# Six small unused transfers among the K and V loads of a one-core decode kernel

## The chip, the core and the metric

The kernel runs on one core of a Trainium2 chip. The metric is device time in microseconds (us). The kernel before was timed three times: 231.49, 231.35 and 231.1 us, so its median is 231.35 us.

## The reference

One token for each of two batch rows goes through a layer norm, and three things are added: the input, an attention with a cached window, and a gated feed-forward block.

```python
xn = _layernorm(x)                                   # x: 2 x 1 x 512
q  = xn @ wq                                         # 32 query heads of 128
k, v = last 4096 rows of k_cache, v_cache            # 2 x 8 heads x 4096 x 128, each for 4 query heads
p  = softmax(q @ k^T * 128 ** -0.5);  o = p @ v
h  = relu(xn @ W_gate) * (xn @ W_up)                 # 1792 wide
out = x + o @ wo + h @ W_down
```

All data is float32. The weights and the used part of the caches are 94.9 MB, each read once.

## The kernel before

Everything large comes through one issuing queue, SP's, in the order of the program text. The helper `load` (line 68) takes a tile from a ring of four slots of 128 x 32 KB and issues one transfer into it (line 70). In the order of its calls it loads: two halves of wq (calls 1 and 2), W_gate (3) and W_up (4), and then one pair of kv heads at a time, 4 MB each: K of group 0 in two parts (5 and 6), and from there K of group g and V of group g-1 by turns (7: K, 8: V, 9: K, 10: V, 11: K, 12: V, 13: K, and so on to call 20). A load waits until the slot that it takes is free, which is when TensorE has read the tile that was there, and until the transfer that filled that slot has landed.

After the loads come W_down (line 99, and two pieces of 128 KB, line 108, whose source pattern at line 106 has KX = 4 as its outermost count), one transfer of 4 MB for the first half of wo and four pieces of 2048, 1280, 512 and 256 KB for the second half (line 497). The program text fixes the order of the instructions on each engine: no scheduler moves them.

TensorE transposes each K tile in 64 steps of 128x128 (line 315), ScalarE and VectorE copy the results out of PSUM by turns (line 304), TensorE forms the scores (line 328). The softmax of the group before (line 334) is interleaved with the transposes of the next K tile, then the product with V follows (line 392). Four groups go through this. At the end W_down and wo are multiplied in as they land (line 479), the sum is copied (line 501) and stored (line 502).

A transfer of 128 rows is spread over the core's 16 DMA engines, here called load engines, eight rows on each. Each engine works through its share of the queue's transfers in order, and a transfer has landed when the last of its engines has finished its share.

Of the kernel before, what the change touches and what calls it, by code (L numbers as in the profile page):

```python
# [9 lines left out]
F32 = mybir.dt.float32  # L10
# [10 lines left out]
def kernel(  # L21
# [12 lines left out]
    nc = tc.nc  # L34
    P = 128
    B, _, D = x.shape
# [21 lines left out]
    const = ctx.enter_context(tc.tile_pool(name="const", bufs=1))  # L58
# [6 lines left out]
    ctx.enter_context(tc.manual_schedule())  # L65


    def load(name, src, shape):
        t = ring.tile(shape, F32, name=name, tag="ring")
        nc.sync.dma_start(t, src)  # L70
        return t


    def load_wq(m):
        src = wq[m * 2 * P:(m + 1) * 2 * P, :].rearrange("(p k) f -> p k f", p=P)
        return load(f"wq{m}", src, [P, 2, HQ * DH])

    def load_ff(w, name):
        return load(name, w.rearrange("(p k) f -> p k f", p=P), [P, KC, F])
# [34 lines left out]
    def load_kv(cache, name, g, a):  # L114
        r, b = divmod(g, B)
        base = cache[b, r * C + 2 * a, SK - W:SK, :]
        run = J * DH
        src = bass.AP(
            tensor=cache.tensor, offset=base.offset, ap=[[run, PK], [SK * DH, 2], [1, run]]
        )  # L120
        return load(f"{name}{g}_{a}", src, [P, run])
# [86 lines left out]
    for kc in range(KC):  # L208
        m, k = divmod(kc, 2)
# [321 lines left out]
```

## Time and profile before

| | us |
|---|---|
| median of three runs | 231.35 |
| the profiled execution | 231.31 |
| its span, first to last instruction | 229.5 |
| TensorE busy | 183.6 |
| VectorE busy | 67.3 |
| ScalarE busy | 48.6 |

The profiled execution takes 231.31 us, of which the span is 229.5 us; 1.81 us lie around it. Core clock: the granted TensorE clock is 0.948 on the mean. The page's DMA line gives, in 40 slices of the span, the busy share of the 16 load engines in tenths. The view by windows gives the same share for any stretch, so a share times 16 times the length of the stretch is load-engine time, and that divided by a count of packets is the time of one. A packet here is one row's piece of a transfer; the records also hold packets of 4 bytes, which post the completion of an engine's share.

### The profile page before, as it was taken

How to read it: one execution, taken by the hardware profiler on the slowest of the kernel's cores; microseconds unless marked ns; L12 is line 12 of the kernel's file. 1: busy time of each engine (PE TensorE's matmuls, PEld its weight loads, DVE VectorE, ACT ScalarE, POOL GpSimd, SP SyncE). 2: the span in 40 equal slices, each digit the busy share in tenths (PEclk: the TensorE clock that was granted, in tenths of full speed). 3: DMA queues.
4: the chain of work that ended last, by engine and by line, in shares of the span. 5: the costliest groups of instructions: out<-in, count | busy, mean ns of one | idle time of the engine just before them, and what ended most of it. 6: DMA issues, size and time to landing. Idle time of an engine off the chain costs nothing.

```text
span 229.5 us, 4147 instructions
## 1 busy us (share of the span) xinstructions
PE 183.6 (80%) x1876; PEld 114.8 (50%) x1876; DVE 67.3 (29%) x135; ACT 48.6 (21%) x82; POOL 7.7 (3%) x24
## 2 busy tenths in 40 slices
PE   0195754829999889998999799599999974988694
PEld 0151222429666573664584565348656533247582
DVE  0500101204544462441472341147224224001000
ACT  2000100004444561540252332025234202010000
POOL 8100000000000000000000000000000300000000
PEclk9999988976999999999999999979999997699889
DMA  7999999999999999999999999999999999999991
GB/s 275 451 428 408 455 405 443 423 448 434 405 443 440 421 411 445 437 417 431 434 440 415 445 417 425 434 428 434 420 445 425 423 428 432 413 448 420 414 367 54
DMA packets 3816, 95.15 MB, mean 415 GB/s; under 512 B 430, under 2 KB 438, under 8 KB 696
## 3 DMA queue, kind: packets, MB, share of 16 engines
q1 hardware_dynamic: 3796, 94.90, 96.7%
q8 instruction: 14, 0.23, 0.4%
q14 instruction: 2, 0.02, 0.0%
q10 hardware_dynamic: 4, 0.00, 0.0%
HBM read 94.90 MB, written 0.00 MB: 413 GB/s over the span
## 4 chain that ended last, share of the span: by engine, by line
PE 53%; DMA 34%; DVE 5%; POOL 2%; ACT 2%; issue 1%; SPq 0%; POOLq 0%
DMA k<-in_A_k_cache_dram 25%; PE pk L315 23%; PE s L328 11%; DMA wo<-in_A_wo_dram 10%; PE o L392 9%; PE q_ps L221 2%; PE pp L372 2%; PE xt_ps L211 2%; ACT p L361 2%; PE oa L408 2%; DVE kT L304 1%; PE y_ps L479 1%; PE op L422 1%; DVE on L304 1%; POOL spread L163 1%
## 5 line engine op out<-in xcount | busy, mean ns | idle before, releaser
L315 PE MATMUL pk<-ident,k 128*128 128x128 f32 x512 | 68.3, 287 | 7.3 <-DMA k<-in_A_k_cache_dram 7.3
L315 PEld LDWEIGHTS pk<-ident,k 128*128 128x128 f32 x512 | 58.1, 146 | 22.1 <-issue 17.9
L304 DVE COPY kT<-pk 128x512 f32<-128x512 f32 x64 | 44.3, 691 | 53.5 <-PE pk L315 43.6
L304 ACT COPY kT<-pk 128x512 f32<-128x512 f32 x64 | 37.5, 586 | 71.7 <-PE pk L315 71.7
L328 PE MATMUL s<-kT,qz 128*32 128x512 f32 x256 | 31.7, 610 | 0.0
L392 PE MATMUL o<-v,pt 128*32 128x512 f32 x256 | 31.6, 626 | 0.0
L392 PEld LDWEIGHTS o<-v,pt 128*32 128x32 f32 x256 | 11.2, 115 | 15.1 <-issue 10.4
L328 PEld LDWEIGHTS s<-kT,qz 128*32 128x32 f32 x256 | 7.2, 111 | 12.7 <-issue 12.3
L211 PE MATMUL xt_ps<-rep,xn 2*128 2x32 f32 x16 | 3.7, 400 | 10.4 <-DVE xn L205 10.4
L479 PE MATMUL y_ps<-wo,oT 128*17 128x128 f32 x256 | 9.5, 310 | 3.0 <-DMA wo<-in_A_wo_dram 3.0
L221 PE MATMUL q_ps<-wq,xnT 128*32 128x512 f32 x64 | 9.2, 727 | 3.3 <-DMA wq<-in_A_wq_dram 2.8
L408 PE MATMUL oa<-on,pick 128*16 128x128 f32 x64 | 8.3, 273 | 4.1 <-DVE on L304 3.3
L304 DVE COPY on<-o 128x512 f32<-128x512 f32 x4 | 2.8, 692 | 29.6 <-PE o L392 29.6
L408 PEld LDWEIGHTS oa<-on,pick 128*16 128x16 f32 x64 | 5.8, 97 | 11.1 <-DVE on L304 7.0
L479 PEld LDWEIGHTS y_ps<-wo,oT 128*17 128x17 f32 x256 | 7.9, 111 | 4.4 <-DMA wo<-in_A_wo_dram 3.9
L211 PEld LDWEIGHTS xt_ps<-rep,xn 2*128 2x128 f32 x16 | 3.6, 319 | 10.4 <-issue 10.4
L304 ACT COPY on<-o 128x512 f32<-128x512 f32 x4 | 2.3, 586 | 26.6 <-PE o L392 26.6
L98 POOL MEMSET wx<- 64x2048 f32 x1 | 1.8, 1804 | 174.5 <-PE s L328 174.5
L372 PE MATMUL pp<-ident,p 128*128 128x128 f32 x32 | 5.5, 306 | 2.4 <-ACT p L361 1.5
L361 ACT ACTIVATE p<-s,nm 128x1024 f32<-128x1024 f32 x4 | 4.5, 1115 | 12.5 <-DVE nm L356 12.5
L221 PEld LDWEIGHTS q_ps<-wq,xnT 128*32 128x32 f32 x64 | 2.2, 130 | 9.5 <-issue 5.2
L249 PE MATMUL g_ps<-wg,xnT 128*32 128x416 f32 x32 | 4.7, 752 | 2.6 <-DMA wg<-in_B_W_gate_dram 2.6
(84 smaller groups left out, 72.7 us busy)
## 6 DMA issues: line engine op xcount, KB each, us to landing
k<-in_A_k_cache_dram SPq DMA_DIRECT2D x8, 4096.0 KB, 28.9
v<-in_A_v_cache_dram SPq DMA_DIRECT2D x8, 4096.0 KB, 27.2
wq<-in_A_wq_dram SPq DMA_DIRECT2D x2, 4096.0 KB, 17.1
wo<-in_A_wo_dram SPq DMA_DIRECT2D x1, 4096.0 KB
wg<-in_B_W_gate_dram SPq DMA_DIRECT2D x1, 3584.0 KB, 29.8
wu<-in_B_W_up_dram SPq DMA_DIRECT2D x1, 3584.0 KB, 38.9
wd<-in_B_W_down_dram SPq DMA_DIRECT2D x1, 3328.0 KB
wo<-in_A_wo_dram SPq DMA_DIRECT2D x1, 2048.0 KB, 19.8
```

Source lines behind the costliest of these rows:

```text
L163: nc.gpsimd.tensor_copy(spread[:, e, :, e], ident[0:HR, 0:HR])
L211: nc.tensor.matmul(xt_ps[:, o, kc, :], cols, rep.rearrange("r s b -> r (s b)"), start=True, stop=True)
L221: nc.tensor.matmul(q_ps[r][32 * c:32 * c + 32, :], xnT[:, 0, kc, :], wqt[kc // 2][:, kc % 2, n * 512:(n + 1) * 512], start=(kc == 0), stop ...
L249: nc.tensor.matmul(dst[32 * c:32 * c + 32, :], xnT[:, 1, kc, :], wt[:, kc, c * MQ:(c + 1) * MQ], start=(kc == 0), stop=(kc == KC - 1),)
L304: (nc.vector.tensor_copy if turn[0] % 2 else nc.scalar.copy)(dst, src)
L315: nc.tensor.transpose(pk[:, u * P:(u + 1) * P], kt_in[:, j * P:(j + 1) * P], ident)
L328: nc.tensor.matmul(ss[g][32 * q:32 * q + 32, :], qz[:, g, 32 * n:32 * n + 32], kt[:, h, q * 512:(q + 1) * 512], start=(a == 0 and s1 == 0 ...
L361: nc.scalar.activation(p, both, AF.Exp, bias=nm, scale=SCALE, accum_out=l)
L372: nc.tensor.transpose(pp[:, u], pv[:, lo:lo + P], ident)
L392: nc.tensor.matmul(o[32 * q:32 * q + 32, :], pts[g][:, jh, n].rearrange("p u k -> p (u k)"), v[:, lo:lo + 512], start=(s1 == 0 and jh == 0 ...
L408: nc.tensor.matmul(oa[g], pick[:, u, 8 - 8 * a:24 - 8 * a], ons[a][:, u], start=(a == 0 and u == 0), stop=(a == NP - 1 and u == 3),)
L479: nc.tensor.matmul(y_ps[32 * e:32 * e + 17, :], lhsT.rearrange("p b s -> p (b s)")[:, 0:17], w[:, e * P:(e + 1) * P], start=False, stop=stop,)
```

## The change

`load` counts its calls. After each of calls 8 to 13 it allocates one more tile in the constant pool and issues one more transfer on the same queue, right behind the load. The six transfers take the first 128, 144, 160, 176, 192 and 208 elements (512, 576, 640, 704, 768 and 832 bytes) of the first 14, 12, 10, 8, 6 and 2 rows of W_down, and write each row to a partition of its own (0, 4, 8 and so on). By the change's description they run over 14, 12, 10, 8, 6 and 2 load engines. Nothing reads the six tiles. Together they are 52 rows and 32,384 bytes; they occupy 4,032 bytes of a partition.

```diff
+    at = [0]
+
     def load(name, src, shape):
         t = ring.tile(shape, F32, name=name, tag="ring")
         nc.sync.dma_start(t, src)
+        at[0] += 1
+        if 8 <= at[0] <= 13:
+            i = at[0] - 8
+            k = (14, 12, 10, 8, 6, 2)[i]
+            run = 128 + 16 * i
+            seen = const.tile([64, run], F32, name=f"seen{i}")
+            nc.sync.dma_start(
+                seen[0:4 * k:4, :], bass.AP(tensor=w_down.tensor, offset=w_down.offset, ap=[[D, k], [1, run]])
+            )
         return t
```

The instructions on TensorE, VectorE, ScalarE and GpSimd are the same ones in the same order; SP issues 35 transfers in place of 29. Completions are counted on eight semaphores taken by turns, so the six transfers move the later loads to other semaphores, and some instructions wait on a semaphore of another number. Where a semaphore comes round again, the next transfer waits for the one that had it: the fifth small transfer waits for the first, the sixth for the second, and calls 15, 17 and 19 and the W_down load wait for the third, fourth, fifth and sixth besides what they waited for before.

## The prediction

> **What bounds the kernel now.** I read the page's DMA row and its queue table first, then the view by windows in six stages and in the last microseconds, then SP's own timeline and waits. The load engines are busy from the second slice of the span to the last but one:
>
> ```profile
> PEclk9999988976999999999999999979999997699889
> DMA  7999999999999999999999999999999999999991
> ...
> q1 hardware_dynamic: 3796, 94.90, 96.7%
> q8 instruction: 14, 0.23, 0.4%
> ```
>
> SP's queue (q1) alone keeps 16 load engines occupied for 96.7% of 229.5 us, which is 221.9 us for each. TensorE, the next, is busy for 183.6 us. The view by windows (columns: stretch, length, busy time of each engine with its instruction count, granted clock, load engines' share, GB/s) says that this holds in every stage and is not only an average:
>
> ```profile
> 2.00:50.00 48.00, 25.22 (x280) 12.55 (x280) 7.50 (x29) 2.24 (x5) 4.47 (x17) 0.96 0.99 426
> 50.00:100.00 50.00, 47.64 (x389) 33.18 (x390) 23.17 (x37) 19.97 (x33) 0.00 (x0) 0.94 1.00 429
> 100.00:150.00 50.00, 44.34 (x380) 27.31 (x378) 17.22 (x30) 13.34 (x23) 0.00 (x0) 0.98 1.00 429
> 150.00:200.00 50.00, 44.50 (x368) 25.37 (x370) 17.78 (x34) 11.76 (x21) 1.80 (x1) 0.92 1.00 429
> ```
>
> From 50 to 200 us the share is 1.00 and the rate 429 GB/s, or 26.8 GB/s for each engine. So the engines never run dry, however long TensorE or SP wait, and time that is added to the busiest engine's work is not taken up by an idle stretch later. The chain of waits on the page gives TensorE 53% and transfers 34%; I do not go by it, because it follows a load back to its issue, and at its issue the engines still had earlier loads to finish.
>
> The end hangs on the load engines too. The drain and what follows it:
>
> ```profile
> 221.00:222.00 1.00, 1.00 (x45) 0.92 (x37) 0.00 (x0) 0.00 (x0) 0.00 (x0) 1.00 0.99 406
> 222.00:223.00 1.00, 1.00 (x47) 1.00 (x39) 0.00 (x0) 0.00 (x0) 0.00 (x0) 1.00 0.75 309
> 223.00:224.00 1.00, 0.32 (x12) 0.04 (x3) 0.00 (x0) 0.00 (x0) 0.00 (x0) 1.00 0.71 274
> 224.00:225.00 1.00, 0.85 (x32) 0.85 (x36) 0.00 (x0) 0.00 (x0) 0.00 (x0) 1.00 0.50 195
> 225.00:225.60 0.60, 0.60 (x24) 0.33 (x20) 0.00 (x0) 0.00 (x0) 0.00 (x0) 1.00 0.22 82
> ```
>
> ```profile
> 226.08 0.13 PEld L479 LDWEIGHTS y_ps<-wo,oT 128*17 128x17 f32 x8 [0.30 <-DMA wo<-in_A_wo_dram]
> 226.56 0.29 DVE L501 COPY yo<-y_ps 128x128 f32<-128x128 f32 x1 [12.30 <-PE y_ps L479]
> 226.88 0.61 SPq L502 DMA_DIRECT2D out_dram<-yo  x1
> ```
>
> The share falls from 0.99 to 0.22 within four microseconds: the 16 engines finish one after another, the first near 222 and the last near 225.5 us. The last eight matmuls (226.08) waited 0.30 us for the last piece of wo, and the copy and the store follow at once. So the time is set by the **latest** load engine, not by the mean of them. The idle share from 222 to 225.6 is (0.25 + 0.29 + 0.50 + 0.78 x 0.6), or 1.5 us for each engine: that is what evening out could give at most, and an engine that finishes early can take extra work for nothing.
>
> **The change part by part.** Nothing is removed. Added are 52 short rows on the load engines, six issues on SP, six tiles, and other semaphores.
>
> *The rows.* An engine gets at most one row of each transfer, so six at most (4,032 bytes) and none at least; the mean is 52/16 = 3.25 rows and 2,024 bytes. Rows this short are not loaded in the kernel before. The nearest packets are these: the 12 of the store (four of them of 4 bytes), in the DMA view of 228.0 to 228.3 us, and the last pieces of wo, in that of 225.0 to 225.6 us:
>
> ```profile
> DMA packets 12, 0.00 MB, mean 14 GB/s; under 512 B 4, under 2 KB 12, under 8 KB 12
> ...
> q1 hardware_dynamic: 12, 0.00, 5.4%
> ```
>
> ```profile
> DMA packets 31, 0.05 MB, mean 82 GB/s; under 512 B 7, under 2 KB 7, under 8 KB 31
> ...
> q1 hardware_dynamic: 31, 0.05, 22.3%
> ```
>
> The first: 5.4% of 16 x 0.3 us is 0.259 us over eight rows of 512 bytes, 0.032 us a row with its part of the completions; 512 bytes at 26.8 GB/s are 0.019 us, so 0.013 us is overhead. The second: 22.3% of 16 x 0.6 us is 2.14 us over 24 rows of 2 KB, 0.089 us a row. An engine with six rows therefore pays 4,032 bytes / 26.8 GB/s = 0.150 us and 6 x 0.013 = 0.08 us, together **0.23 us**. Bounds for one engine: 0 (it has no row) and 6 x 0.089 = 0.53 us (each row as dear as one of 2 KB). I take 0.23 us, since 512 bytes are nearer to these rows than 2 KB, and I let it count in full, as if the latest engine were one with five or six rows. The reason for that is in the code: the two W_down pieces have 4 as the outermost count of their source (line 106), so I take it that they load four engines with 64 KB each that the others do not have, 2.4 us at 26.8 GB/s, and that these are among the latest. If the latest has none of the rows, the change costs nothing there.
>
> [...] No view of the profile numbers the engines.
>
> *SP's issues.* A load's issue takes 0.53 to 0.54 us on SP; the six new ones stand right behind those of calls 8 to 13:
>
> ```profile
> 44.94 0.54 SPq L70 DMA_DIRECT2D v<-in_A_v_cache_dram  x1
> 60.90 0.54 SPq L70 DMA_DIRECT2D k<-in_A_k_cache_dram  x1
> 72.31 0.54 SPq L70 DMA_DIRECT2D v<-in_A_v_cache_dram  x1
> 86.89 0.54 SPq L70 DMA_DIRECT2D k<-in_A_k_cache_dram  x1
> 92.21 0.53 SPq L70 DMA_DIRECT2D v<-in_A_v_cache_dram  x1
> 101.94 0.54 SPq L70 DMA_DIRECT2D k<-in_A_k_cache_dram  x1
> 108.13 0.54 SPq L70 DMA_DIRECT2D v<-in_A_v_cache_dram  x1
> ```
>
> The shortest distance to the next load is 86.89 to 92.21, 5.3 us, in which SP waits for TensorE's use of a slot. One more issue of about 0.54 us fits into each, so I put it at nothing; without that cover six would be 3.2 us of issue, still ahead of engines with work queued.
>
> *The waits by semaphore.* The fifth small transfer waits for the first, the sixth for the second, four later loads for the other four. Each lands with the load ahead of it:
>
> ```profile
> k<-in_A_k_cache_dram SPq DMA_DIRECT2D x8, 4096.0 KB, 28.9
> v<-in_A_v_cache_dram SPq DMA_DIRECT2D x8, 4096.0 KB, 27.2
> ```
>
> The closest case is the sixth, issued near 102.5: the second went out near 61.4 and lands by about 60.90 + 28.9 = 89.8. That is 12 us early, so nothing waits. No load is given a wait on a later large load.
>
> *The tiles.* Nothing reads them. They move other tiles to other addresses; transfers and instructions keep their shapes, so I put that at nothing.
>
> The sum against the profiled execution is 231.31 + 0.23 = 231.54 us. Its 231.31 is 0.04 under the median of 231.35, within the 0.39 us that the three runs span. Prediction **231.55 us**, 0.1% up. What a measurement of this kernel can tell from no change is about 0.2%, or 0.46 us.
>
> **The rivals.**
>
> *A small transfer holds its engine longer than its bytes (slower).* If an engine had to wait out a small row's read or its completion before it went on, each would cost a round trip. The row for it is q8 in the page's table: 14 instruction blocks of 16 KB took 0.4% of 16 x 229.5 us, about 1.05 us each, where 16 KB at 26.8 GB/s are 0.61 us. So a transfer that comes between others can cost 0.44 us over its bytes. Six of these are 2.6 us: 234 us. It would decide from about 0.08 us a row. Against it: the share stays at 0.99 from 221 to 222 us, while the engines pass from one piece of wo to the next, so a change of transfer on this queue opens no such gap.
>
> [...] I give this whole rival 0.12.
>
> *The instruction blocks fall on other engines (slower or faster).* TensorE's program comes in over the same load engines, in 14 blocks. A block on an engine that would finish among the latest moves the end by the block's 1.05 us. If the change shifts which engine takes a block, the likely case is one more block on a late engine: 231.35 + 0.23 + 1.05 = 232.6 us. It decides only if the choice depends on the time or on the other queue's state; the three runs before lie within 0.39 us, which speaks for a fixed choice. Slower this way: 0.16. The other way, a late engine is spared a block: at most the 1.5 us of evening out, and since several engines are late together, about half of it, so 230.6 us or a little more. Faster: 0.08.
>
> *The rows are hidden.* The latest engine has none of them or few; then the time stays at 231.35 us. This lies within the same 0.2% as the forecast, and the two share the chance below.
>
> **How the numbers follow.** Forecast, with the hidden case: 0.64, between 231.1 and 231.9 us (the three runs' spread below, 0.53 us above). In it I leave 0.07 for slower by over 0.2%, where the rows near their upper bound, and 0.01 for faster by a shift between builds. Small transfers dear 0.12, a block on a late engine 0.16, a block spared 0.08. So faster 0.09, within 0.2% 0.56, slower 0.35. The range reaches from 231.1 to 232.7 us: it takes in the forecast and the block on a late engine, and leaves out most of the dear transfers and of the faster case. The likeliest case by itself is 231.1 to 231.9 us.
>
> **What would show it.** In the changed kernel q1 should show 52 more data packets and some 0.03 MB more, the windows from 50 to 200 us should stay at a share of 1.00 and 429 GB/s, and SP's issues of calls 14 and later should come at the same times within a few tenths. The last wo matmuls should start 0.0 to 0.5 us after 226.08. I am wrong if the share dips behind the small transfers (then they are dear), if the drain from 222 to 225.6 us is shorter or longer by a microsecond while the stretch ahead of it is the same (then the blocks or something else went to other engines), or if the rate of 429 GB/s itself changes, for which I have no mechanism.

## The result, and the profile after

The changed kernel takes 231.78 us (median of 12 runs, 231.52 to 231.93) against 231.37 us for the kernel before in the same runs (231.1 to 231.8). The ratio is 1.0016, with a 95% interval of 1.0008 to 1.0023: 0.37 us slower, with 0.19 to 0.53 us as the interval. The forecast was 0.2 us slower and within 0.2%. The profiled execution takes 231.91 us, with a span of 230.1 us.

The page of the changed kernel, its DMA row, packets and queues:

```profile
DMA  7999999999999999999999999999999999999981
...
DMA packets 3920, 95.18 MB, mean 414 GB/s; under 512 B 482, under 2 KB 542, under 8 KB 800
...
q1 hardware_dynamic: 3900, 94.93, 96.6%
q8 instruction: 14, 0.23, 0.4%
```

q1 has 104 packets more than the 3796 of before: 52 rows and 52 completions (the count under 512 bytes is up by 52, from 430). It moved 0.03 MB more. The instruction blocks are still 14, at the same share. The stages, in the view by windows (length, busy time by engine, granted clock, load engines' share, GB/s):

```profile
50.00:100.00 50.00, 47.37 (x384) 32.94 (x385) 22.62 (x38) 19.78 (x33) 0.00 (x0) 0.93 1.00 429
100.00:150.00 50.00, 44.45 (x383) 27.54 (x383) 17.73 (x30) 13.39 (x24) 0.00 (x0) 0.99 1.00 429
150.00:200.00 50.00, 44.50 (x364) 25.03 (x366) 17.77 (x34) 11.87 (x21) 1.80 (x1) 0.91 1.00 430
...
222.00:223.00 1.00, 1.00 (x44) 1.00 (x40) 0.00 (x0) 0.00 (x0) 0.00 (x0) 1.00 0.87 360
223.00:224.00 1.00, 0.64 (x24) 0.36 (x16) 0.00 (x0) 0.00 (x0) 0.00 (x0) 1.00 0.66 264
224.00:225.00 1.00, 0.47 (x20) 0.47 (x24) 0.00 (x0) 0.00 (x0) 0.00 (x0) 1.00 0.64 244
225.00:226.00 1.00, 1.00 (x40) 0.73 (x32) 0.00 (x0) 0.00 (x0) 0.00 (x0) 1.00 0.27 100
```

Share and rate from 50 to 200 us are those of before: no dip where the small rows pass. Only the drain lies later. The last matmuls, the copy and the store, in order of time:

```profile
226.46 0.13 PEld L490 LDWEIGHTS y_ps<-wo,oT 128*17 128x17 f32 x8 [0.31 <-DMA wo<-in_A_wo_dram]
226.94 0.29 DVE L512 COPY yo<-y_ps 128x128 f32<-128x128 f32 x1 [12.20 <-PE y_ps L490]
227.26 0.61 SPq L513 DMA_DIRECT2D out_dram<-yo  x1
```

Each of the three is 0.38 us later than before (226.08, 226.56, 226.88), and the last matmuls still wait for wo. But one pair of executions does not price the small rows: in this one call 9 already went out at 61.42 us in place of 60.90, before the first small row had moved. In a second profile of the changed kernel ("the change again" below) it went out at 59.01 us, 1.89 us earlier than before, and yet the last matmuls started at 226.29, 0.21 us later than before. So the loss is read from the medians. The next fences show a small row's own price, in DMA views of the changed kernel 2 ns wide, each with a single packet: one of 512 bytes at 78.069 us and one of 832 bytes at 126.854 us.

```profile
DMA packets 1, 0.00 MB, mean 256 GB/s; under 512 B 0, under 2 KB 1, under 8 KB 1
...
q1 hardware_dynamic: 1, 0.00, 84.4%
```

```profile
DMA packets 1, 0.00 MB, mean 416 GB/s; under 512 B 0, under 2 KB 1, under 8 KB 1
...
q1 hardware_dynamic: 1, 0.00, 121.9%
```

A share counts the packet's whole time, so 84.4% of 16 x 2 ns is 27 ns and 121.9% is 39 ns. Read in the same way, packets of 576, 640, 704 and 768 bytes took 29, 32, 34 and 36 ns. One of each makes 197 ns; the six completions, 9 ns each, make 54 ns. An engine with all six rows pays **0.25 us**, one with the first five 0.20 us.

### The profile page after: what moved, and what is told of

Read it like the earlier page. It is cut to its first block, busy times and chain, and to the rows that moved or that the text cites. A ratio compares the mean times of both kernels' runs of the same rounds, so it can differ in the third digit from the quotient of the medians.

```text
span 230.1 us, 4153 instructions
## 1 busy us (share of the span) xinstructions
PE 186.7 (81%) x1876; PEld 115.0 (50%) x1876; DVE 67.2 (29%) x135; ACT 48.5 (21%) x82; POOL 7.7 (3%) x24
## 4 chain that ended last, share of the span: by engine, by line
PE 54%; DMA 34%; DVE 5%; POOL 2%; ACT 2%; issue 1%; SPq 0%; POOLq 0%
DMA k<-in_A_k_cache_dram 25%; PE pk L326 23%; PE s L339 11%; DMA wo<-in_A_wo_dram 10%; PE o L403 9%; PE q_ps L232 3%; PE pp L383 2%; PE xt_ps L222 2%; ACT p L372 2%; PE oa L419 2%; DVE kT L315 1%; PE y_ps L490 1%; PE op L433 1%; DVE on L315 1%; POOL spread L174 0%
## 5 line engine op out<-in xcount | busy, mean ns | idle before, releaser
L232 PE MATMUL q_ps<-wq,xnT 128*32 128x512 f32 x64 | 11.1, 858 | 3.0 <-DMA wq<-in_A_wq_dram 2.5
L260 PE MATMUL u_ps<-wu,xnT 128*32 128x416 f32 x32 | 5.6, 884 | 5.8 <-DMA wu<-in_B_W_up_dram 5.8
## 6 DMA issues: line engine op xcount, KB each, us to landing
k<-in_A_k_cache_dram SPq DMA_DIRECT2D x8, 4096.0 KB, 27.8
```

The lines of the kernel that those rows point to most:

```text
L232: nc.tensor.matmul(q_ps[r][32 * c:32 * c + 32, :], xnT[:, 0, kc, :], wqt[kc // 2][:, kc % 2, n * 512:(n + 1) * 512], start=(kc == 0), stop ...
L260: nc.tensor.matmul(dst[32 * c:32 * c + 32, :], xnT[:, 1, kc, :], wt[:, kc, c * MQ:(c + 1) * MQ], start=(kc == 0), stop=(kc == KC - 1),)
```

## The experiments

Theory 1 is the prediction's: the load engines never idle, the end is set by the latest of them, and a row costs its few tens of ns there and nothing elsewhere. Against it stood: that moved addresses or the build make a part of the 0.37 us (2), that a transfer costs something wherever it lands (3), and that the mean work of the engines counts (4). All differences below are against the kernel before, run on the same chip beside each kernel, and come from the ratio and its interval.

**Tiles alone, one element written.** The transfer in the diff of the change is replaced:

```diff
-            nc.sync.dma_start(seen[0:4 * k:4, :], ...)
+            nc.gpsimd.memset(seen[0:1, 0:1], 0.0)
```

> The six tiles are kept, the six transfers are left out; GpSimd writes one element of each tile. Theory 1 (the time is the last load engine's, and only rows on it count): no change from before, within 0.1 us. Theory 2 (part of the change's 0.4 us comes from the moved addresses or the build, since the profile after is already 0.17 us behind before the first small row): 0.1 to 0.25 us slower than before.

Measured: 231.61 us against 231.45, ratio 1.0006 (0.9997 to 1.0015), 0.14 us slower (0.07 faster to 0.35 slower). The interval takes in what theory 1 and what theory 2 expected, so this decides nothing between them; a kernel whose tiles nothing touches stands further below.

**Nine transfers over two, four and sixteen engines.** Behind calls 8 to 16, rows of 768 bytes in place of the six transfers; K is 2, 4 or 16 (the counter and the line that allocates the tiles are left out):

```diff
...
+        if 8 <= at[0] <= 16:
+            i = at[0] - 8
+            nc.sync.dma_start(seen[i // 2][2 * (i % 2):2 * (i % 2) + 4 * K - 3:4, :],
+                bass.AP(tensor=w_down.tensor, offset=w_down.offset, ap=[[D, K], [1, 192]]))
```

> Nine transfers of 768-byte rows behind calls 8 to 16, on two load engines each: 0.40 us more on each of the two (9 x (36 + 9) ns by the packet records after). Theory 1: the packet records put the last of the four engines that carry the W_down pieces some 0.45 us behind the next of them, and that one had five rows in the changed kernel and so is not one of the two that had six; so the rows stay hidden, 0 to 0.1 us slower. Theory 3 (any transfer costs the same wherever it lands, by its issue or its completion): 9/6 of the change's 0.4 us, 0.6 us slower. Theory 4 (the mean work of the engines counts): 0.05 us.

> The same nine transfers on four load engines each, the number that the W_down pieces use. Theory 1: the last engine is among them and pays in full, 0.40 us slower than before. Theory 3: 0.6 us, the same as on two. Theory 4: 0.10 us.

> The same nine transfers on all sixteen load engines. Theory 1: 0.40 us slower, the same as on four, though four times the rows. Theory 3: 0.6 us. Theory 4: 0.40 us, four times the run on four engines.

| engines | median, us | range of 11 runs | ratio (95%) | slower by, us |
|---|---|---|---|---|
| 2 | 231.40 | 231.29 to 231.56 | 0.9997 (0.9988 to 1.0006) | -0.07 (-0.28 to 0.14) |
| 4 | 231.79 | 231.58 to 231.96 | 1.0010 (1.0001 to 1.0019) | 0.23 (0.02 to 0.44) |
| 16 | 232.00 | 231.66 to 232.26 | 1.0018 (1.0009 to 1.0027) | 0.42 (0.21 to 0.62) |

The pages count 18, 36 and 144 packets under 512 bytes more than the 430 of before, one completion for each added row. Two engines carry nine rows more and the time does not move; on four engines it does, and the two ranges of runs don't meet. Both kernels issue the same nine transfers, so theory 3 falls: 0.6 us was expected of each. On four and on sixteen engines 0.40 us was expected, and both intervals take it in; the 0.19 us between the two is less than the intervals' width. Theory 4's 0.05, 0.10 and 0.40 us fit these three runs as well; the long rows decide about it.

**Long rows, with four engines late and with four engines early.** Three kernels: one adds nine transfers of four rows of 4,032 bytes; one sets KX from 4 to 8, which gives the last 128 rows of W_down to eight engines with 32 KB each (the page counts 438 packets under 512 bytes, eight completions more than before), and adds no rows; one does both.

```diff
...
+            nc.sync.dma_start(seen[4 * i:4 * (i + 1), :],
+                bass.AP(tensor=w_down.tensor, offset=w_down.offset, ap=[[3 * D, 4], [1, 1008]]))
...
-    KX = 4
+    KX = 8
```

> Nine transfers of rows of 4,032 bytes on four load engines each: 9 x (4,032 / 26.8 ns + 17 ns) = 1.51 us more on each of the four. Theory 1: 1.5 us slower than before, one for one. Theory 4 (mean of the engines): 0.38 us. If a transfer costs by its number and not by its bytes: 0.4 to 0.6 us, as with short rows.

> The kernel before with KX = 8 in place of 4: the last 128 rows of W_down go to eight load engines with 32 KB each in place of four with 64 KB, and no small transfers. Theory 1: the four engines finish 1.2 us earlier, and the last is then one that took two instruction blocks, 0.12 us before the old end: 0 to 0.2 us faster than before. If one of the four engines that now get 32 KB is such an engine: 1.1 us slower.

> The nine long transfers on four engines, in the kernel with KX = 8. Theory 1: the first four engines have 1.2 us of room there, so of the 1.51 us some 0.3 us shows: 0.2 to 0.4 us slower than before, 1.2 us less than the same rows with KX = 4. If the rows cost wherever the end is set: 1.4 to 1.5 us over the run with KX = 8 alone.

| kernel | median, us (before: 231.44) | ratio (95%) | slower by, us |
|---|---|---|---|
| long rows, KX = 4 | 233.73 | 1.0103 (1.0089 to 1.0117) | 2.38 (2.06 to 2.71) |
| KX = 8 alone | 231.26 | 0.9992 (0.9978 to 1.0006) | -0.19 (-0.51 to 0.14) |
| long rows, KX = 8 | 232.64 | 1.0051 (1.0037 to 1.0066) | 1.18 (0.86 to 1.53) |

The same rows cost 1.20 us less where the four engines have 32 KB less to do, and 32 KB at 26.8 GB/s are 1.22 us: room on an engine takes up its own rows one for one, as far as intervals of 0.3 us to each side can tell. KX = 8 alone gains at most 0.51 us of these 1.22, so other engines finish close behind the four. And both runs with long rows are 0.9 us dearer than expected.

**The same long rows, four partitions apart.**

```diff
-                seen[4 * i:4 * (i + 1), :],
+                seen[32 * (i // 4) + i % 4:32 * (i // 4) + i % 4 + 13:4, :],
```

> Nine rows of 4,032 bytes on each of four load engines again, but a transfer's four rows go to partitions four apart, as the small rows of the change do, in place of four neighbours. If the neighbours made the 2.3 us of the first such run (four engines writing into one group of partitions at once): 1.5 us slower than before, the bytes alone. If long rows on few engines are dear wherever they are written: 2.3 us again.

Measured: 232.83 us against 231.46, ratio 1.0060 (1.0047 to 1.0074), 1.39 us slower (1.09 to 1.71), where bytes alone would make 1.51. So the 0.9 us of the first run came from where the rows were written (the run with KX = 8 was not repeated with rows apart). Theory 1's price holds for the rows when they are written apart; theory 4's 0.38 us does not. The view by windows of this kernel shows the few late engines by themselves at the end:

```profile
224.00:225.00 1.00, 0.71 (x28) 0.43 (x16) 0.00 (x0) 0.00 (x0) 0.00 (x0) 1.00 0.59 236
225.00:226.00 1.00, 0.23 (x8) 0.23 (x12) 0.00 (x0) 0.00 (x0) 0.00 (x0) 1.00 0.34 131
226.00:227.00 1.00, 1.00 (x40) 0.78 (x30) 0.00 (x0) 0.00 (x0) 0.00 (x0) 1.00 0.11 41
227.00:228.00 1.00, 0.97 (x28) 0.48 (x24) 0.00 (x0) 0.00 (x0) 0.00 (x0) 1.00 0.01 4
```

After 226 us the share is 0.11, under two engines' worth, and the kernel waits for those.

**The change again, its rows with no address moved, and its tiles with no row.** The second keeps the six transfers, but their tiles lie in a pool behind all others; the third allocates the tiles and never touches them, which moves 91 of 119 tiles as the change does.

```diff
# rows, no address moved
+    late = ctx.enter_context(tc.tile_pool(name="late", bufs=1))
-            seen = const.tile([64, run], F32, name=f"seen{i}")
+            seen = late.tile([64, run], F32, name=f"seen{i}")
# tiles, no row
-            seen = const.tile([64, run], F32, name=f"seen{i}")
-            nc.sync.dma_start(seen[0:4 * k:4, :], ...)
+            const.tile([64, run], F32, name=f"seen{i}")
```

> The changed kernel once more, beside the two that follow. All theories: 0.2 to 0.5 us slower than before, as in the first measurement (0.37 us by the ratio).

> The six small transfers as in the changed kernel, but their tiles lie in a pool behind all others, so that every other tile keeps the address it has in the kernel before. Theory 1 (rows on the last engine alone): 0.20 to 0.25 us slower than before (five rows on the last engine cost 0.20 us by the packet records, six 0.24 us), the same as the changed kernel within 0.1 us. Theory 2 (a part comes from moved addresses): 0.1 to 0.2 us less than the changed kernel.

> The six tiles are allocated and never touched: no transfer and no instruction more than before, but 91 of 119 tiles lie 4,032 or 1,728 bytes higher, as in the changed kernel. Theory 1: no change, within 0.1 us. Theory 2: 0.1 to 0.25 us slower than before, as the run with one element written per tile (0.14 us by its ratio) could suggest.

| kernel | median, us (before: 231.46) | ratio (95%) | slower by, us |
|---|---|---|---|
| the change again | 231.84 | 1.0016 (1.0007 to 1.0025) | 0.37 (0.16 to 0.58) |
| rows, no address moved | 231.82 | 1.0013 (1.0004 to 1.0021) | 0.30 (0.09 to 0.49) |
| tiles, no row | 231.48 | 1.0002 (0.9993 to 1.0011) | 0.05 (-0.16 to 0.25) |

With no address moved the rows make a loss by themselves, 0.30 us, which can't be told from the 0.37 us of the change. The tiles alone make none that can be measured. So nothing is left for theory 2 to explain; the interval of the tiles alone still leaves room for up to 0.25 us. The last matmuls on wo, in order of time, first with the rows and no address moved, then with the tiles and no row:

```profile
226.38 0.13 PEld L491 LDWEIGHTS y_ps<-wo,oT 128*17 128x17 f32 x8 [0.30 <-DMA wo<-in_A_wo_dram]
```

```profile
226.13 0.13 PEld L486 LDWEIGHTS y_ps<-wo,oT 128*17 128x17 f32 x8 [0.30 <-DMA wo<-in_A_wo_dram]
```

These two executions differ by 0.25 us, which agrees with the price of an engine's rows but does not prove it: executions of the first kernel alone lie between 231.52 and 232.10 us.

**A version that evens the engines out.** KX = 8 as above, and FM from 13 to 12, so that 256 rows of W_down go to eight engines and every engine gets 16 KB less of the rest (again 438 packets under 512 bytes).

> The kernel before with KX = 8 and FM = 12: 256 rows of W_down go to the first eight engines, and every engine gets 16 KB less of the rest. By theory 1 the engines that took two instruction blocks finish 0.6 us earlier and the first eight 0.6 us later than the last of them with KX = 8 alone, if none of the eight took a block too many: 0.1 to 0.5 us faster than before. If one of them did: up to 1 us slower.

Measured: 231.15 us against 231.44, ratio 0.9986 (0.9972 to 1.0001), 0.32 us faster (0.65 faster to 0.02 slower). It is the lowest median here and leans the way that was expected, but its interval reaches no change, so it is not shown to beat the kernel before.

## Why the prediction was right, step by step

*What bounds the kernel.* Right. With 0.40 us more on two engines nothing moved; with some 1.5 us more on four late ones the kernel lost 1.39 us. A mean share of 1.00 did not say this: the drain did. The packet records of the trace say it too. All packets of the queue, with the instruction blocks, join into 16 rows in which each packet starts within a few ns of the end of the one ahead of it, mostly 3 or 4 ns before it. Each of the 16 holds 152 of the 2,432 packets of 32 KB, eight of every load in the order of the issues, and a packet of 4 bytes behind every eight. So each load engine's packets can be followed one after another, and on the engine that ends last no gap opens from the first load to the last piece of wo, neither before nor after. Before the change the last of the 16 completions of wo ends at 225.57 us, and the last eight matmuls start at 226.08.

*The price of the rows.* Right: 0.23 us was forecast for six rows, from the 512-byte packets of the store, and the packets show 0.25 us. Over its bytes a row cost 17 ns, 8 in its own packet and 9 in its completion, where 13 had been taken. The choice of the store's packets over the 2 KB packets (0.53 us) was good. The measured loss is 0.37, 0.30 and again 0.37 us, somewhat over the 0.20 us of five rows and the 0.25 us of six, but each interval takes both in. Whether a tenth or two of a microsecond are missing from the sum stays open.

*Which engines pay.* Right as to the four that carry the W_down pieces: two engines are hidden, four are not, and giving the four 1.2 us of room takes 1.2 us off the price of their rows. The prediction had this from the code alone, with no view that named the latest engine. Followed packet by packet in the changed kernel's trace, the engine that ends last carried eight rows of 8 KB of the W_down pieces, as three others did, and five of the six small rows (512 to 768 bytes), so 0.20 us is its price. No engine carried two rows of one small transfer. An engine without W_down pieces ends only 0.05 us ahead of it, and 0.13 us ahead in the trace of before: the four are the latest by little.

*SP's issues.* Hidden as said, but mis-sized. I took 0.54 us; the changed kernel's own rows show 0.67 to 0.94 us:

```profile
61.42 0.56 SPq L72 DMA_DIRECT2D k<-in_A_k_cache_dram  x1
62.03 0.81 SPq L79 DMA_DIRECT2D seen<-in_B_W_down_dram  x1
...
87.41 0.55 SPq L72 DMA_DIRECT2D k<-in_A_k_cache_dram  x1
88.01 0.70 SPq L79 DMA_DIRECT2D seen<-in_B_W_down_dram  x1
92.73 0.55 SPq L72 DMA_DIRECT2D v<-in_A_v_cache_dram  x1
```

The issue of twelve rows took SP 0.81 us and that of 128 rows 0.56 us. In the shortest stretch SP is done at 88.71 and issues next at 92.73, so 4.0 us of cover were left.

*The waits and the tiles.* Right: call 9, which has no wait added, goes out 0.52 us later than before, and calls 15, 17 and 19 and the W_down load, which have one, go out 0.53, 0.44, 0.48 and 0.48 us later, so no semaphore held one; and the tiles alone cost nothing that can be measured.

*The rivals.* Dear transfers are ruled out: 144 rows on sixteen engines cost 0.42 us in all, where 0.44 us for each transfer would have been 4 us. That the blocks of instructions fell on other engines is not needed: their number and share are the same, and the engine that ends last, followed packet by packet, took none of the 14 blocks, neither before nor after. No view numbers the engines, so where each block fell was not tested by itself. That the blocks are TensorE's program was the author's reading; what the trace of before shows of it is their pace, one after 150 to 444 more matmuls and weight loads, 259 on the mean. The rival's price was too low: beside a block's own 1.05 us, the eleven load packets of 32 KB that came right behind one before the change took 1.68 to 1.76 us in place of 1.22, so a block cost its engine about 1.5 us.

## What to carry to other kernels

Where load engines are busy from end to end, ask which of them finishes last, not how busy they are on the mean: here 0.40 us more on two others was free, and on the last ones 32 KB less, 1.22 us at the engine's rate, took 1.20 us off the price of their rows. The drain in the view by windows, a share falling from 0.99 to 0.22 in four microseconds before the change, shows the slack. The number of engines that a transfer is spread over shifted work from one engine to another (KX = 8 in place of 4), though no version here was shown to be faster for that. Price a small row by the shortest packets of the same trace, here bytes over the engine's 26.8 GB/s plus 17 ns with the completion, and not by a transfer's time from issue to landing, 27.8 us on the median for a load of K in the changed kernel.

## What the runs showed of the hardware that was not expected

Nine transfers of four rows of 4,032 bytes cost 2.38 us when a transfer's rows were written to four neighbouring partitions, and 1.39 us when written four partitions apart; the intervals (2.06 to 2.71 and 1.09 to 1.71) don't meet. One packet of each kernel, in DMA views 2 ns wide, the longest among neighbours (at 108.983 us) and the longest of those apart (at 157.996 us):

```profile
q1 hardware_dynamic: 1, 0.00, 953.1%
```

```profile
q1 hardware_dynamic: 1, 0.00, 525.0%
```

That is 305 ns against 168 ns for the same bytes. Most rows took 156 to 165 ns in both kernels, though, so the rows' own time does not hold the 0.9 us. The large packets of the loads do. From 77 to 165 us, a stretch that holds all 36 rows in both kernels, the queue is equally busy and moves 0.20 MB less with neighbours (first line) than apart (second line), six packets of 32 KB:

```profile
q1 hardware_dynamic: 1353, 37.40, 99.8%
```

```profile
q1 hardware_dynamic: 1359, 37.60, 99.8%
```

A 32 KB packet of a load took 1.22 us on the median in the trace of before. Of the 36 that came right behind a long row and its completion, 22 took 1.25 to 1.55 us with neighbours and two (up to 1.29 us) with rows apart. The engine that ended last with neighbours carried nine of them, which took 1.13 us more than nine usual ones would, about the 0.99 us between the two runs. What holds them up is not shown.

And a small transfer took SP longer to issue than the loads of K and V beside it, 0.53 to 0.57 us: 0.94 us for the fourteen rows of the change, 0.70 us for eight and 0.67 us for two. The number of rows alone did not set this: with rows of 768 bytes sixteen took 0.60 us, four 0.65 and two 0.64.
